# More blocks of an MLP by a seven-product scheme, both batches in turn to the last block

## The chip, the cores and the metric

One core of a Trainium2 chip runs the whole program. The time is the device time of one execution in microseconds (us); lower is better. Three runs of the kernel before gave a median of 463.32 us, from 462.43 to 463.98.

## The reference

Two batches of 768 tokens go through three parts. First a decaying linear attention over 8 heads of 64. Then a layer norm and an MLP whose result is added to its input. Then a mixture of four attention heads of width 64 of which each token uses two.

```
state = gamma * state + outer(k_t, v_t);  y_t = scale * q_t @ state      # 8 heads, 768 steps
xn = (x - mu) / sqrt(var + 1e-6) * g_ln
x  = x + maximum(xn @ w_ch1, 0) @ w_ch2                                   # 512 -> 2048 -> 512
logits = x @ w_gate;  w = softmax over the two largest of four
for e in range(4):
    q, k, v = x @ wq[e], x @ wk[e], x @ wv[e]
    a = softmax(causal(q @ k.T / 8))
    out += (weight of e) * (a @ v @ wo[e])
```

## The kernel before, in words

Everything is written as nodes of a plan (`P.add`): each has the engine, an estimated duration, what it reads and writes, and a priority, which is its place in the program plus `P.bias`. `P.issue` then runs a list scheduler over these estimates: at every step an engine that is free takes the ready node of the smallest priority number whose buffers have a place. The order that comes out is the order of the instructions on each engine, DMA issues on SP's queue included. A node that is ready late by the estimates is simply ordered later, and other work goes ahead of it.

Three stages follow each other. In the first (up to about 70 us) `r_tile` does the linear attention and the layer norm in 12 tiles of 128 tokens. Tokens are then kept transposed, features on partitions, in two halves of 384 tokens per batch (`j` = 0, 1): `xT` in fp32, and `XH` and `XL`, a rounded high part and the rest, since each product of full precision is done as three matmuls (high by high, high by low, low by high).

The second stage is the MLP, in eight blocks `f` of 256 hidden columns. For each block `m_h` makes the hidden values of one batch and one half in two groups of 12 matmuls of 128x384 (L576), ACT and DVE split the result (L579, L580), and `m_c` adds the block's part to `xT`: 6 matmuls (L595) and one DVE add (L598) for each of four groups of features. In the last block `m_c` also splits the new `xT` into `XH` and `XL` (L601, L603). The weights arrive as four pieces of 512 KB per block in 64-bit floats; `split_piece` turns them into fp32 on ACT, POOL and DVE (L508 to L514) and splits them (L532, L533), eight pieces ahead. Buffers of the weights hold two blocks.

Blocks in `SEVEN` (3, 4 and 5) use another way for the first product, `m_h7`: for one batch it takes both token halves and both weight halves as a 2x2 block product and makes the four results with seven products of 6 matmuls (L654) where `m_h` has eight. It needs sums of weight blocks (`w_sums`, L548 to L551, into two `S` buffers per block, of which four places exist, one shared with a `raw` buffer of the arriving weights) and sums of token blocks (`x_sums`, 12 POOL instructions L616, L619, L623 per batch, made once). Partial results are kept and added on ACT and DVE (L661, L665). The `m_c` groups of the batch before are put between the seven products.

The third stage: `load_mw` brings in wk, wq, wv and wo and splits them (L711 to L713); `q_proj` (L738) makes queries and keys, `q_val` (L775) values and gate logits, of batch 0 and later of batch 1; `a_scores`, `a_value`, `a_out` are the attention. `q_phase(1)` is there to fill the gaps of batch 0's attention.

Before, blocks 0 to 5 go through both batches in turn, and blocks 6 and 7 first for batch 0, then for batch 1. The loads of wk, wq, wv and wo are put into the plan at steps 20 to 23, in block 5, and wait for the last `m_h7`. `x_sums(0)` and `x_sums(1)` are put in at the first step of block 1 and of block 2, with a bias of 150.

Of the kernel before, what the change touches and what calls it, by code (L numbers as in the profile page):

```python
# [41 lines left out]
NB = S // TB  # L42
# [2 lines left out]
NFC = FF // FC  # L45
NPC = 4
LATE = 150
SEVEN = (3, 4, 5)
NEG = -1000000000.0
LIMIT = float(np.array(0x0FEFFFFF, np.uint32).view(np.float32))  # L50

# [155 lines left out]
def region(base, size, n, space="S"):  # L207
    return [(space, base + i * size, size) for i in range(n)]
# [3 lines left out]
def retention_channel_mlp_mixture_attention(ctx: ExitStack, tc: tile.TileContext, a):  # L212
# [71 lines left out]
    PL["u"] = region(o_u, 3 * KB // 2, 3) + region(o_w + 28 * KB, 3 * KB // 2, 2)  # L284
    PL["xT"] = region(o_xt, 6 * KB, 4)
    PL["x"] = region(o_x, 6 * KB, 8)
    x = o_r
    for n, size in (("wq", 4 * KB), ("wk", 4 * KB), ("wv", 4 * KB + 16), ("wo", 4 * KB)):
        PL[n] = region(x, size, 2)
        x += 2 * size  # L290
    PL["mraw"] = region(x, 4 * KB + 16, 2)
    PL["qk0"] = region(x, 3 * KB, 12)
    PL["vv0"] = region(x + 36 * KB, KB, 6)
    x += 42 * KB
    PL["ob"] = region(x, 2 * KB, 1) if x + 2 * KB <= o_h else []
    assert x <= o_h
    PL["qk1"] = region(o_h, 3 * KB, 12)
    PL["vv1"] = region(o_h + 36 * KB, KB, 6)
    PL["ob"] += region(o_h + 42 * KB, 2 * KB, 1)
    PL["pr"] = region(o_xt, 3 * KB, 8)  # L300
    PL["pt"] = region(o_x, 6 * KB, 3)
    PL["at"] = region(o_x + 18 * KB, 2 * KB, 3)
# [238 lines left out]
    def w_sums(f, y0, y1):  # L541
        t, h, l = new("sf"), new("S"), new("S")
        part = lambda i: f32(t)[:, 256 * i:256 * i + 256].rearrange("p (k c) -> p k c", k=2)
        for i, p, q, op in ((0, lambda: half_of(y0, 1), lambda: half_of(y1, 1), OP.add),
                            (1, lambda: part(0), lambda: half_of(y0, 0), OP.subtract),
                            (2, lambda: half_of(y0, 0), lambda: half_of(y0, 1), OP.subtract),
                            (3, lambda: half_of(y1, 0), lambda: part(1), OP.subtract)):
            P.add({"V": 0.45, "G": 0.8}, lambda e, i=i, p=p, q=q, op=op: (dve if e == "V" else pool).tensor_tensor(  # L548
                part(i), p(), q(), op), r=[y0, y1] + [(t, n) for n in {1: [0], 3: [1]}.get(i, [])], w=[(t, i)])
        ACT(1.1, lambda: act.activation(f32r(h), f32(t), AF.Copy), r=[(t, i) for i in range(4)], w=[h])  # L550
        P.add({"V": 1.2, "G": 2.4}, lambda e: (dve if e == "V" else pool).tensor_tensor(f32r(l), f32(t), f32(h), OP.subtract),  # L551
              r=[h] + [(t, i) for i in range(4)], w=[l])
        W[f, "S"] = (h, l)

    def w1_at(f, k, m):
        i, k = divmod(k, 2)
# [68 lines left out]
    def m_h7(f, b, rest):  # L625
        a11, (y1h, y1l), (sh, sl) = W[f, 0][0], W[f, 1], W[f, "S"]

        def weights(n):
            if n == "a11":
                return [a11], lambda k: (f32r(a11)[:, k * 128:(k + 1) * 128], f32r(a11)[:, 256 + k * 128:256 + (k + 1) * 128])  # L630
            h, l = (sh, sl) if n[0] == "s" else (y1h, y1l)
            c0 = 256 * int(n[1]) if n[0] == "s" else 128 * int(n[1])
            step = 128 if n[0] == "s" else FC
            return [h, l], lambda k: tuple(f32r(t)[:, c0 + k * step:c0 + k * step + 128] for t in (h, l))

        def tokens_of(n):
            if n[0] == "t":
                h, l = TH[b][int(n[1])], TL[b][int(n[1])]
                return [h, l], lambda k: tuple(f32r(t)[:, k * TB:(k + 1) * TB] for t in (h, l))
            kh, j = int(n[1]), int(n[2])  # L640
            h, l = XH[b][j], XL[b][j]
            return keys(h) + keys(l), lambda k: tuple(blk(f32r(t))[:, 2 * kh + k] for t in (h, l))

        def product(pa, wn, xn, first):
            wr, wat = weights(wn)
            xr, xat = tokens_of(xn)

            def mm():
                n = 0
                for k in range(2):  # L650
                    wh, wl = wat(k)
                    xh, xl = xat(k)
                    for wt, t in ((wh, xh), (wh, xl), (wl, xh)):
                        pe.matmul(f32(pa, TB), lhsT=wt, rhs=t, start=(first and n == 0), stop=(n == 5), skip_group_check=True)  # L654
                        n += 1
            r = [(t, z) for t in wr for z in (0, 1)] if wn == "a11" else list(wr)
            PE(1.04, mm, r=r + xr, w=[pa])

        def keep(pa):
            u = new("u")  # L660
            ACT(0.49, lambda: act.activation(f32(u), f32(pa, TB), AF.Copy), r=[pa], w=[u])  # L661
            return u

        def add(dst, pa, u):
            DVE(0.55, lambda: dve.tensor_tensor(f32(dst, TB), f32(pa, TB), f32(u), OP.add), r=[pa, u], w=[dst])  # L665

        def out(src):
            h, l = new("h"), new("h")
            ACT(0.49, lambda: act.activation(f32r(h, TB), f32(src, TB), AF.Relu), r=[src], w=[h])
            DVE(0.55, lambda: dve.scalar_tensor_tensor(f32r(l, TB), f32(src, TB), 0.0, f32(h, TB), op0=OP.max,  # L670
                                                       op1=OP.subtract), r=[src, h], w=[l])
            return h, l

        pa, pb, pc = (new("ps") for _ in range(3))
        def go_on(n=1):
            for _ in range(min(n, len(rest))):
                m_c(*rest.pop(0))

        product(pa, "a11", "x00", True)
        c1 = keep(pa)  # L680
        product(pb, "s1", "t1", True)
        add(pb, pb, c1)
        go_on()
        product(pa, "y0", "x10", False)
        h00 = out(pa)
        u2 = keep(pb)
        go_on()
        product(pc, "s0", "t0", True)
        go_on()
        product(pb, "s2", "t2", False)  # L690
        u3 = keep(pb)
        c22 = new("u")
        add(c22, pc, u3)
        go_on()
        product(pb, "y1", "t3", False)
        h10 = out(pb)
        go_on()
        product(pc, "s3", "x11", False)
        add(pc, pc, u2)
        h01 = out(pc)  # L700
        h11 = out(c22)
        P.writer["sums"] = P.nodes[-1]
        return [h00, h10], [h01, h11]

    MW = {}

    def load_mw(n):
        raw, h, l = new("mraw"), new(n), new(n)
        w = E * HD + E if n == "wv" else E * HD
        sz = NK * w  # L710
        DMA(sz * 512, lambda: sp.dma_start(f32(raw, sz), a[n].rearrange("p k n -> p (k n)")), r=["sums"], w=[raw])  # L711
        ACT(1.05, lambda: act.activation(f32r(h, sz), f32(raw, sz), AF.Copy), r=[raw], w=[h])
        POOL(2.4, lambda: pool.tensor_tensor(f32r(l, sz), f32(raw, sz), f32(h, sz), OP.subtract), r=[raw, h], w=[l])  # L713
        MW[n] = (h, l, DM if n == "wo" else w)
# [14 lines left out]
    def q_proj(b, j, n, p):  # L729
# [3 lines left out]
        for hf in range(2):  # L733
            def mm(hf=hf):
                i = 6 * hf
                for k in (2 * hf, 2 * hf + 1):
                    for lo, xt in ((0, xh), (0, xl), (1, xh)):
                        pe.matmul(f32(pa, TB), lhsT=mw(n, lo, k, p * 128, (p + 1) * 128), rhs=blk(f32r(xt))[:, k],  # L738
                                  start=(i == 0), stop=(i == 11))
                        i += 1  # L740
            PE(0.98, mm, r=list(MW[n][:2]) + xkeys(xh) + xkeys(xl), w=[pa])
        for z in range(2):
            e = 2 * p + z
            own = slice(64 * z, 64 * z + 64)
# [200 lines left out]
    DMA(8e3, lambda: sp.dma_start(before, a["before"]), w=["before"])  # L945
    DVE(0.1, lambda: dve.memset(negs, NEG), w=["negs"])
    steps = []
    for f in range(NFC - 2):
        steps += [(f, b, j) for j, b in (((0, 0), (0, 1), (1, 0), (1, 1)) if f == 0 else ((0, 0), (1, 0), (0, 1), (1, 1)))]
    for b in range(B):  # L950
        steps += [(f, b, j) for f in (NFC - 2, NFC - 1) for j in range(NB)]
    nxt = 8
    rest = []

# [4 lines left out]
    for n, (f, b, j) in enumerate(steps):  # L959
        for _ in range(2 if f >= NFC - 2 else 1):  # L960
            if nxt == len(pieces):
                break
            load_piece(*pieces[nxt])
            split_piece(*pieces[nxt])
            nxt += 1
        if (f, b, j) in ((1, 0, 0), (2, 0, 0)):
            P.bias += LATE
            x_sums(f - 1)
            P.bias -= LATE
        if n in (20, 21, 22, 23):  # L970
            load_mw(("wk", "wq", "wv", "wo")[n - 20])
        if f not in SEVEN:
            flush()
            hh = m_h(f, b, j)
            rest = [(f, b, j, hh, k) for k in range(NK)]
        elif j == 1:
            hs = m_h7(f, b, rest)
            flush()
            rest = [(f, b, jj, hh, k) for jj, hh in enumerate(hs) for k in range(NK)]

    flush()

    def q_phase(b):
# [83 lines left out]
```

## Time and profile before

| what | value |
|---|---|
| median of three runs | 463.32 us |
| the profiled execution | 464.56 us, its span 462.8 us |
| instructions | 8255 |
| DVE busy | 315.7 us (68%) |
| ACT busy | 217.4 us (47%) |
| POOL busy | 201.3 us (44%) |
| granted TensorE clock | 0.998 of full speed |
| PE's share of the chain that ended last | 86% |
| L595 and L576, shares of that chain | 27% and 18% |

The span is what lies between the first and the last instruction of the profile. PE is a matmul, PEld the load of its weights, which overlaps it; DVE, ACT and POOL are the vector, scalar and GpSimd engines, SP issues the DMAs. L595 is line 595 of the kernel as printed above.

### The profile page before, as it was taken

The numbers are of one execution on the slowest core, as the hardware profiler recorded it, in microseconds if no ns is written. First come the engines' busy times: TensorE is split into PE (matmuls) and PEld (weight loads), VectorE is DVE, ScalarE is ACT, GpSimd is POOL, SyncE is SP. The second block draws the span as 40 slices with busy tenths as digits, with TensorE's granted clock in tenths as the row PEclk, the third lists the DMA queues.
The fourth block names the chain that finished last, engine by engine and source line by source line (L and its number), as shares of the span: only waits on it lengthen the run. The fifth ranks groups of instructions, "written<-read, shape, count | busy, mean of one in ns | idle before, by whom it ended". The sixth has DMA issues, their size and how long they took to land.

```text
span 462.8 us, 8255 instructions
## 1 busy us (share of the span) xinstructions
PE 450.2 (97%) x3117; PEld 424.5 (92%) x3117; DVE 315.7 (68%) x671; ACT 217.4 (47%) x458; POOL 201.3 (44%) x209
## 2 busy tenths in 40 slices
PE   4999999999999999999999999999999999999996
PEld 4888899999999999999999999999899988898774
DVE  2697878667659559779988344443547888778962
ACT  0576685362255136255455212303434767745862
POOL 1588779889885123334145602202100514224440
PEclk9999999999999999999999999999999999999999
DMA  7899820333004005014214100000220231101111
GB/s 261 310 333 341 321 96 31 108 105 99 24 17 165 3 0 182 3 44 139 91 47 142 43 0 2 0 1 0 69 61 10 65 72 47 45 2 47 45 47 45
DMA packets 14983, 40.08 MB, mean 87 GB/s; under 512 B 2272, under 2 KB 4960, under 8 KB 14944
## 3 DMA queue, kind: packets, MB, share of 16 engines
q1 hardware_dynamic: 14944, 39.57, 25.3%
q8 instruction: 24, 0.39, 0.4%
q14 instruction: 15, 0.12, 0.1%
HBM read 33.27 MB, written 3.15 MB: 79 GB/s over the span
## 4 chain that ended last, share of the span: by engine, by line
PE 86%; DMA 3%; DVE 3%; ACT 3%; POOL 2%; issue 2%; SPq 0%; POOLq 0%; DVEq 0%; ACTq 0%
PE ps L595 27%; PE ps L576 18%; PE ps L654 8%; PE ps L738 6%; PE ps L891 4%; PE ps L775 4%; PE ps L880 4%; PE ps L910 4%; PE ps L838 2%; PE ps L839 2%; DMA raw<-in_w_dram 2%; PE ps L472 2%; PE ps L428 2%; PE ps L447 2%; PE ps L440 1%
## 5 line engine op out<-in xcount | busy, mean ns | idle before, releaser
L595 PE MATMUL ps<-h,w 128*128 128x384 f32 x768 | 141.8, 335 | 1.2 <-DVE xT L598 0.5
L595 PEld LDWEIGHTS ps<-h,w 128*128 128x128 f32 x768 | 133.6, 188 | 2.4 <-DVE xT L598 0.8
L598 DVE TENSOR_TENSOR xT<-xT,ps 128x384 f32<-128x384 f32 x128 | 69.7, 551 | 31.9 <-PE ps L595 31.6
L576 PE MATMUL ps<-x,w 128*128 128x384 f32 x480 | 86.8, 335 | 0.0
L576 PEld LDWEIGHTS ps<-x,w 128*128 128x128 f32 x480 | 83.3, 188 | 0.0
L860 POOL TENSOR_SCALAR pr<-pr,sm,gate 128x384 f32<-128x384 f32 (+5 forms) x48 | 34.8, 734 | 83.5 <-DVE ps L845 34.6
L579 ACT ACTIVATE h<-ps 128x384 fp32r<-128x384 f32 x40 | 19.6, 491 | 76.1 <-PE ps L576 76.1
L533 POOL TENSOR_TENSOR w<-wy,w 128x512 fp32r<-128x512 f32 x29 | 37.6, 1307 | 40.6 <-ACT w L532 22.2
L580 DVE SCALAR_TENSOR_TENSOR h<-ps,h 128x384 fp32r<-128x384 f32 x40 | 22.1, 556 | 42.3 <-ACT h L579 42.3
L848 ACT ACTIVATE pr<-ps,sm 128x384 f32<-128x384 f32 (+5 forms) x48 | 30.3, 635 | 16.6 <-DVE sm L846 10.5
L603 POOL TENSOR_TENSOR x<-xT,x 128x384 fp32r<-128x384 f32 x11 | 11.2, 1017 | 56.5 <-ACT x L601 56.3
L509 POOL TENSOR_SCALAR wx<-wx 128x512 f32<-128x512 f32 x32 | 20.2, 632 | 34.4 <-ACT wx L508 32.0
L508 ACT ACTIVATE wx<-raw 128x512 f32<-128x512 f32 x32 | 21.5, 672 | 27.4 <-DVE ps L512 16.6
L846 DVE TENSOR_REDUCE sm<-ps 128x1 f32<-128x384 f32 (+5 forms) x48 | 30.0, 625 | 2.8
L532 ACT ACTIVATE w<-wy 128x512 fp32r<-128x512 f32 x29 | 17.8, 627 | 11.1 <-PE ps L595 8.1
L512 DVE SCALAR_TENSOR_TENSOR ps<-wx,ps 128x512 uint32<-128x512 uint32 x32 | 22.2, 693 | 0.9
L514 DVE SCALAR_TENSOR_TENSOR wy<-raw,ps 128x512 uint32<-128x512 uint32 x32 | 21.7, 683 | 1.3 <-POOL w L533 0.6
L510 DVE TENSOR_SCALAR ps<-wx 128x512 uint32<-128x512 uint32 x32 | 22.0, 687 | 0.8
L880 PE MATMUL ps<-ident,pr 128*128 128x128 f32 x168 | 22.0, 275 | 0.1
L432 DVE TENSOR_TENSOR am<-ps,caus 128x512 f32<-128x512 f32 x24 | 15.6, 684 | 9.3 <-PE ps L428 9.1
L838 PE MATMUL ps<-qk,qk 128*128 128x512 f32 (+3 forms) x64 | 21.7, 347 | 0.2 <-ACT pr L848 0.2
L654 PE MATMUL ps<-t,S 128*128 128x384 f32 x108 | 21.5, 334 | 0.0
(115 smaller groups left out, 803.9 us busy)
## 6 DMA issues: line engine op xcount, KB each, us to landing
raw<-in_w_dram SPq DMA_DIRECT2D x32, 512.0 KB, 3.6
vk<-in_vk_dram SPq DMA_DIRECT2D x12, 512.0 KB, 5.6
kq<-in_kq_dram SPq DMA_DIRECT2D x11, 512.0 KB, 6.1
qk<-qk SPq DMA_DIRECT2D x32, 96.0 KB, 2.1
out_dram<-ob SPq DMA_DIRECT2D x11, 256.0 KB, 2.0
tabY<-in_tabY_dram SPq DMA_DIRECT2D x6, 256.0 KB, 5.1
mraw<-in_wv_dram SPq DMA_DIRECT2D x1, 520.0 KB, 3.3
kq<-in_kq_dram SPq DMA_DIRECT2D x2, 256.0 KB, 3.2
```

Source lines behind the costliest of these rows:

```text
L512: DVE(0.7, lambda: dve.scalar_tensor_tensor(u32(z), u32(x), 0x80000000, u32(z), op0=OP.bitwise_and, op1=OP.bitwise_or), r=[x, z], w=[z])
L533: POOL(1.34, lambda: pool.tensor_tensor(f32r(l), f32(y), f32(h), OP.subtract), r=[y, h], w=[l])
L576: pe.matmul(f32(pa, TB), lhsT=wt, rhs=blk(f32r(xt[b][j]))[:, k], start=(n == 0), stop=(n == 11))
L595: pe.matmul(f32(pa, TB), lhsT=wt, rhs=t, start=(n == 0), stop=(n == 5))
L598: DVE(0.55, lambda k=k, pa=pa: dve.tensor_tensor(blk(f32(xt))[:, k], blk(f32(xt))[:, k], f32(pa, TB), OP.add), r=[pa] + keys(xt), w=[(xt, ...
L654: pe.matmul(f32(pa, TB), lhsT=wt, rhs=t, start=(first and n == 0), stop=(n == 5), skip_group_check=True)
L738: pe.matmul(f32(pa, TB), lhsT=mw(n, lo, k, p * 128, (p + 1) * 128), rhs=blk(f32r(xt))[:, k], start=(i == 0), stop=(i == 11))
L838: pe.matmul(f32(s)[:, n0:n1], lhsT=q, rhs=f32r(KH[b, e])[:, n0:n1], start=True, stop=False)
L846: dve.tensor_reduce(f32(sm)[:, z:z + 1], f32(s, nk), axis=AX, op=OP.max, negate=True)
L848: ACT(act_c(nk) + .18, lambda s=s, pr=pr, z=z: act.activation(f32(pr, nk), f32(s, nk), AF.Exp, bias=f32(sm)[:, z:z + 1], scale=1.0, accum_ ...
L860: POOL(0.28 + nk * 0.95e-3, lambda pr=pr, z=z, e=e: pool.tensor_scalar(f32(pr, nk), f32(pr, nk), f32(sm)[:, 6 + z:7 + z], GT[b, j][:, cc, ...
L880: pe.transpose(f32(pa)[:, i * C:(i + 1) * C], f32(PRS[z][x])[:, j * C:(j + 1) * C], ident)
```

## The change

`SEVEN` becomes blocks 2 to 7. The steps are f = 0 to 7, in each of them both batches. `x_sums` of batch 0 is put in within block 0 and that of batch 1 at the start of block 1, with the same bias. wk and wq are put in at two steps of block 7 and wait for the last block's weight sums; wv and wo are put in behind the last step and wait for the last `m_h7` (key `"seven"`), and so does every `q_proj`. The third stage's buffers get other places, since token and weight sums now live to the end: wk, wq and wo share six places, wv's two parts lie where the raw loads of the others lie, and wv's raw load lies on the `u` buffers.

```diff
@@ -45,7 +45,7 @@
 NFC = FF // FC
 NPC = 4
 LATE = 150
-SEVEN = (3, 4, 5)
+SEVEN = (2, 3, 4, 5, 6, 7)
 NEG = -1000000000.0
 LIMIT = float(np.array(0x0FEFFFFF, np.uint32).view(np.float32))
 
@@ -284,19 +284,17 @@
     PL["u"] = region(o_u, 3 * KB // 2, 3) + region(o_w + 28 * KB, 3 * KB // 2, 2)
     PL["xT"] = region(o_xt, 6 * KB, 4)
     PL["x"] = region(o_x, 6 * KB, 8)
-    x = o_r
-    for n, size in (("wq", 4 * KB), ("wk", 4 * KB), ("wv", 4 * KB + 16), ("wo", 4 * KB)):
-        PL[n] = region(x, size, 2)
-        x += 2 * size
-    PL["mraw"] = region(x, 4 * KB + 16, 2)
-    PL["qk0"] = region(x, 3 * KB, 12)
-    PL["vv0"] = region(x + 36 * KB, KB, 6)
-    x += 42 * KB
-    PL["ob"] = region(x, 2 * KB, 1) if x + 2 * KB <= o_h else []
-    assert x <= o_h
+    slots = region(o_r + 48 * KB, 4 * KB, 6)
+    for n in ("wk", "wq", "wo"):
+        PL[n] = slots
+    x = o_h - 2 * (4 * KB + 16)
+    PL["wv"] = PL["mraw"] = region(x, 4 * KB + 16, 2)
+    PL["vraw"] = region(o_u, 4 * KB + 16, 1)
+    PL["qk0"] = region(o_r, 3 * KB, 12)
+    PL["vv0"] = region(o_r + 36 * KB, KB, 6)
+    PL["ob"] = region(o_r + 42 * KB, 2 * KB, 2)
     PL["qk1"] = region(o_h, 3 * KB, 12)
     PL["vv1"] = region(o_h + 36 * KB, KB, 6)
-    PL["ob"] += region(o_h + 42 * KB, 2 * KB, 1)
     PL["pr"] = region(o_xt, 3 * KB, 8)
     PL["pt"] = region(o_x, 6 * KB, 3)
     PL["at"] = region(o_x + 18 * KB, 2 * KB, 3)
@@ -551,6 +549,7 @@
         P.add({"V": 1.2, "G": 2.4}, lambda e: (dve if e == "V" else pool).tensor_tensor(f32r(l), f32(t), f32(h), OP.subtract),
               r=[h] + [(t, i) for i in range(4)], w=[l])
         W[f, "S"] = (h, l)
+        P.writer["sums"] = P.nodes[-1]
 
     def w1_at(f, k, m):
         i, k = divmod(k, 2)
@@ -699,16 +698,16 @@
         add(pc, pc, u2)
         h01 = out(pc)
         h11 = out(c22)
-        P.writer["sums"] = P.nodes[-1]
+        P.writer["seven"] = P.nodes[-1]
         return [h00, h10], [h01, h11]
 
     MW = {}
 
     def load_mw(n):
-        raw, h, l = new("mraw"), new(n), new(n)
+        raw, h, l = new("vraw" if n == "wv" else "mraw"), new(n), new(n)
         w = E * HD + E if n == "wv" else E * HD
         sz = NK * w
-        DMA(sz * 512, lambda: sp.dma_start(f32(raw, sz), a[n].rearrange("p k n -> p (k n)")), r=["sums"], w=[raw])
+        DMA(sz * 512, lambda: sp.dma_start(f32(raw, sz), a[n].rearrange("p k n -> p (k n)")), r=["seven" if n in ("wv", "wo") else "sums"], w=[raw])
         ACT(1.05, lambda: act.activation(f32r(h, sz), f32(raw, sz), AF.Copy), r=[raw], w=[h])
         POOL(2.4, lambda: pool.tensor_tensor(f32r(l, sz), f32(raw, sz), f32(h, sz), OP.subtract), r=[raw, h], w=[l])
         MW[n] = (h, l, DM if n == "wo" else w)
@@ -738,7 +737,7 @@
                         pe.matmul(f32(pa, TB), lhsT=mw(n, lo, k, p * 128, (p + 1) * 128), rhs=blk(f32r(xt))[:, k],
                                   start=(i == 0), stop=(i == 11))
                         i += 1
-            PE(0.98, mm, r=list(MW[n][:2]) + xkeys(xh) + xkeys(xl), w=[pa])
+            PE(0.98, mm, r=list(MW[n][:2]) + xkeys(xh) + xkeys(xl) + ["seven"], w=[pa])
         for z in range(2):
             e = 2 * p + z
             own = slice(64 * z, 64 * z + 64)
@@ -945,10 +944,8 @@
     DMA(8e3, lambda: sp.dma_start(before, a["before"]), w=["before"])
     DVE(0.1, lambda: dve.memset(negs, NEG), w=["negs"])
     steps = []
-    for f in range(NFC - 2):
+    for f in range(NFC):
         steps += [(f, b, j) for j, b in (((0, 0), (0, 1), (1, 0), (1, 1)) if f == 0 else ((0, 0), (1, 0), (0, 1), (1, 1)))]
-    for b in range(B):
-        steps += [(f, b, j) for f in (NFC - 2, NFC - 1) for j in range(NB)]
     nxt = 8
     rest = []
 
@@ -963,12 +960,12 @@
             load_piece(*pieces[nxt])
             split_piece(*pieces[nxt])
             nxt += 1
-        if (f, b, j) in ((1, 0, 0), (2, 0, 0)):
+        if (f, b, j) in ((0, 0, 1), (1, 0, 0)):
             P.bias += LATE
-            x_sums(f - 1)
+            x_sums(f)
             P.bias -= LATE
-        if n in (20, 21, 22, 23):
-            load_mw(("wk", "wq", "wv", "wo")[n - 20])
+        if n in (28, 30):
+            load_mw("wk" if n == 28 else "wq")
         if f not in SEVEN:
             flush()
             hh = m_h(f, b, j)
@@ -978,6 +975,8 @@
             flush()
             rest = [(f, b, jj, hh, k) for jj, hh in enumerate(hs) for k in range(NK)]
 
+    load_mw("wv")
+    load_mw("wo")
     flush()
 
     def q_phase(b):
```

## Rows read from the trace of the kernel before

**Rows 1.** The page: busy time of the engines, share of the span, instructions.
```profile
PE 450.2 (97%) x3117; PEld 424.5 (92%) x3117; DVE 315.7 (68%) x671; ACT 217.4 (47%) x458; POOL 201.3 (44%) x209
```
**Rows 2.** Windows: PE, PEld, DVE, ACT, POOL busy (instructions), clock, DMA share, GB/s.
```profile
126.90:161.30 34.40, 34.40 (x201) 34.37 (x200) 24.21 (x41) 13.96 (x25) 17.49 (x15) 1.00 0.18 62
161.30:194.20 32.90, 32.59 (x188) 32.27 (x187) 25.31 (x45) 14.53 (x29) 10.40 (x10) 1.00 0.19 64
194.20:227.00 32.80, 32.30 (x187) 31.98 (x186) 26.50 (x45) 16.05 (x32) 10.64 (x11) 1.00 0.29 96
227.00:259.90 32.90, 32.80 (x189) 32.51 (x188) 25.82 (x48) 16.62 (x30) 16.09 (x11) 1.00 0.25 81
259.90:291.00 31.10, 31.10 (x181) 31.10 (x181) 12.11 (x22) 6.54 (x13) 5.99 (x6) 1.00 0.01 2
```
**Rows 3.** Pieces of the chain of waits: start, length, line.
```profile
81.32 6.24 PE ps L576 x36
...
165.58 1.04 PE ps L654 x6
```
**Rows 4.** Waits of PE and PEld: total, times, longest, in us.
```profile
PE ps L595 <- DVE xT L598: 0.5, 1, 0.5
...
PE ps L595 <- DVE h L670: 0.3, 1, 0.3
```
**Rows 5.** Groups of instructions of DVE that the seven products add.
```profile
L665 DVE TENSOR_TENSOR ps<-ps,u 128x384 f32<-128x384 f32 x12 | 6.7, 561 | 1.2 <-PE ps L654 1.2
...
L551 DVE TENSOR_TENSOR S<-sf,S 128x1024 fp32r<-128x1024 f32 x2 | 3.0, 1500 | 0.0
```
**Rows 6.** Instructions of line 548: duration min/median/max in ns, first and last start.
```profile
L548 DVE TENSOR_TENSOR sf<-sf,wy x3: 1054/1392/1395, 141.5 to 209.8; 128x256 f32<-128x256 f32 x3
...
L548 DVE TENSOR_TENSOR sf<-wy,sf x3: 409/416/716, 142.9 to 211.2; 128x256 f32<-128x256 f32 x3
```
**Rows 7.** Timeline: start, length, line; token sums, second block and first seven products.
```profile
72.63 1.84 POOL L616 TENSOR_TENSOR t<-x,x 128x768 f32<-128x768 f32 x1
...
105.71 3.65 POOL L623 TENSOR_TENSOR t<-t,t 128x768 fp32r<-128x768 f32 x2
...
124.84 4.32 PE L576 MATMUL ps<-x,w 128*128 128x384 f32 x24
...
142.99 2.07 POOL L623 TENSOR_TENSOR t<-t,t 128x768 fp32r<-128x768 f32 x1
```
**Rows 8.** Timeline between blocks 3 and 4: release of a weight sum's buffer.
```profile
185.77 1.20 PE L654 MATMUL ps<-x,S 128*128 128x384 f32 x6
...
186.88 2.40 POOL L551 TENSOR_TENSOR S<-sf,S 128x1024 fp32r<-128x1024 f32 x1 [0.93 <-PE ps L654]
...
189.93 1.20 PE L654 MATMUL ps<-t,S 128*128 128x384 f32 x6
```
**Rows 9.** Timeline: end of the MLP, first values of batch 0.
```profile
326.75 2.38 PE L595 MATMUL ps<-h,w 128*128 128x384 f32 x12 [0.29 <-DVE qk L757]
...
338.18 1.72 PE L775 MATMUL ps<-wv,x 128*128 128x260 f32 x12
```
**Rows 10.** Loads of the third stage: landing in us, splits, differences of the last block.
```profile
mraw<-in_wv_dram SPq DMA_DIRECT2D x1, 520.0 KB, 3.3
...
L712 ACT ACTIVATE wv<-mraw 128x1040 fp32r<-128x1040 f32 x1 | 1.1, 1077 | 0.9 <-DMA mraw<-in_wv_dram 0.9
...
L713 POOL TENSOR_TENSOR wv<-mraw,wv 128x1040 fp32r<-128x1040 f32 x1 | 2.4, 2427 | 0.9 <-ACT wv L712 0.9
...
L713 POOL TENSOR_TENSOR wo<-mraw,wo 128x1024 fp32r<-128x1024 f32 x1 | 2.4, 2399 | 1.3 <-ACT wo L712 1.3
...
L603 POOL TENSOR_TENSOR x<-xT,x 128x384 fp32r<-128x384 f32 x11 | 11.2, 1017 | 56.5 <-ACT x L601 56.3
```
**Rows 11.** Windows of line 738 alone, first scores to first transposes: PE, PEld.
```profile
353.30:368.70 15.40, 12.34 (x66) 11.58 (x66) 1.00 0.14 33
```

## The prediction

> **What bounds the kernel now.** The page comes first. PE is busy for 97% of the span and PEld for 92%, DVE for 68% [rows 1], so the first question is whether DVE or a wait bounds PE in some stage. The windows answer it stage by stage: from 126.9 to 161.3 us PE and PEld are busy for the whole stretch, in the three windows to 259.9 us, where the seven products run, PE misses 0.31, 0.50 and 0.10 us, and from 259.9 to 291 us it misses nothing while DVE has 12.11 us of work in 31.10 [rows 2]. Next the chain of waits, to see that these busy times are the engine at its pace: 36 matmuls in a row take 6.24 us and 6 take 1.04, with L576 as with L654 [rows 3], 0.1733 us each. Of PE's waits in the MLP the longest are on DVE, 0.5 us for an add and 0.3 us for a hidden value [rows 4]. So in the blocks that change, a matmul less is 0.173 us less, as long as no new wait opens.
>
> **What goes.** For one batch `m_h` has 48 matmuls in a block (2 halves, 2 groups, 12 each), `m_h7` has 42. Blocks 2, 6 and 7 change, two batches each: 3 x 2 x 6 = 36 matmuls, just the piece of 6.24 us [rows 3]. I take -6.24 us.
>
> **What the three blocks get.** ACT has 6 copies to `u` more per block and one copy of sums, POOL trades one difference of 512 columns for two of 256; neither is near its limit in rows 2. DVE gets 6 adds at 0.561 us, 3.4 us, then the weight sums, and the low part of these at 1.50 us [rows 5]. The sums: three adds between 0.41 and 1.39 us each [rows 6], so 1.2 to 4.2 us. Per block that is 3.4 + 1.5 + 1.2 to 4.2 = 6.1 to 9.1 us; the sums come one block ahead. Block 2: 24.21 + 3.4 = 27.6 of 34.40 - 2.08 = 32.3 us, the sums for block 3 being in that window already. Block 5, which now makes the sums for block 6: 25.82 + 2.7 to 5.7 = 28.5 to 31.5 of 32.9 us. Block 6 has room, 12.11 in 31.10 us for batch 0 alone [rows 2]. DVE stays under PE everywhere, but bursts let PE wait, as the three windows with seven products show: 0.91 us in all. I take the same again for the three new blocks, +0.91 us; one end is 3 x 0.50 = 1.5 us, the other -0.91, if with the new order of the plan the old gaps go too (the window before them, with one block's sums in it, loses nothing).
>
> The Trainium skill says on this ("SBUF — State Buffer", section "Who interferes with whom") that a VectorE instruction with two SBUF inputs excludes a GpSimd instruction that reads SBUF and the reverse, for the whole instruction. This trace agrees: the same shape takes 409 ns at best and 1395 at worst [rows 6]. By that rule alone each of the four two-input instructions of a block's sums could wait for one token sum of 1.84 us [rows 7], 7.4 us of DVE; where that would end is the first rival.
>
> **The buffers of the weight sums.** `S` has four places, one shared with a weight load, so the next block's low part waits until the last product of the block before has read its own. Between blocks 3 and 4 one sees it: the product at 185.77 us, the low part on POOL at 186.88 for 2.40 us after a wait on PE, and the first product that reads it at 189.93 [rows 8]. It is done at 189.28, with 0.65 us to spare, because `m_c` groups and a product that needs no sums lie between. The change makes two more such turns, into block 3 and into block 6; for block 7 no weight load holds the shared place. I take 0 for each, by that row; the other end is a low part with nothing ahead of it, 2.40 us each.
>
> **The token sums.** All 24 POOL instructions must now end before blocks that start one block (some 33 us) sooner. Before, batch 0's start at 72.63 us and end at 109.36; block 2's products start in the middle of the piece at 124.84, at 126.9 [rows 7]. So batch 0 has 17 us to spare. Batch 1's last ends at 145.06 [rows 7]. Its seven products follow 7 products and 8 `m_c` groups of 1.04 us after 126.9, at 142.5, and the first that reads a token sum comes a product later, near 143.5, and reads the second of four sums; the fourth is read by the sixth product, near 150. With the queueing as it was the loss would be at most 1.5 us; queued sooner, ahead of block 3's differences, I take 0. The reverse, POOL's tile work being held up by a token sum, is bounded by one of 1.84 us; PE was busy with products of block 0 there, so 0.
>
> **The end of the MLP.** Batch 0's queries could start before, but the plan started them only as the last product groups ended: the MLP's last matmuls are at 326.75 us, and the first values of batch 0 at 338.18 [rows 9]. So that batch 0 was finished early was hardly used, and little is lost by waiting for `"seven"`: behind the last product PE has 8 `m_c` groups, 8.3 us, for which the hidden values of the first half are long ready, and then 8 `q_proj` of 2.08 us, 16.6 us. Behind these 24.9 us lie the loads of wv and wo, which come late now: 3.3 us to landing, 1.08 us for the high part, then, since wo's raw load has taken the second of wv's two places, wo's difference of 2.40 us and wv's of 2.43 [rows 10]; with wo's own landing behind wv's I make it 11 to 12 us. Even if POOL first does the 8 differences of batch 1's last block at 1.02 us [rows 10], it is 20 us. SP's queue has only transfers of keys behind these issues, which are no earlier. wk and wq are loaded in block 7, with POOL nearly idle. I take 0, between -0.3 (the wait at 326.75 goes [rows 9]) and the price of the third rival.
>
> **Sum.** -6.24 + 0.91 = -5.33 us. Against the profiled execution, 464.56 us with 1.76 us of it outside the span, that is 459.2; this execution lay 1.24 us above the median of 463.32, so the predicted median is 458.0 us. With the ends of the small terms it is 463.32 - 6.24 - 0.91 - 0.3 = 455.9 to 463.32 - 6.24 + 1.5 (blocks) + 1.5 (token sums) = 460.1; the turns of `S` are the first rival.
>
> **Rivals.** First, weight sums come too late: both new turns of `S` lose their 2.40 us, because DVE and POOL hold each other up in the sums (the short add was lengthened to more than three times [rows 6]). -5.33 + 4.8 = -0.5, 462.8 us, no measurable change. For it: only 0.65 us to spare [rows 8]. Against it: no wait of PE on a weight sum is among its waits in three blocks. That is where the Trainium skill's rule on the shared port would end.
>
> Second, the time is given back in part: the list scheduler orders the third stage anew, and PE loses 2 to 3 us among scores and transposes, 460.5 us. For it: DVE has little slack there. Against it: the stage's work is the same.
>
> Third, slower: the values of batch 0 come late. Until gates and values are there no transposes and value products can go, and PE uses the queries and keys of batch 1 meanwhile. These were the filling between the first scores and the first transposes, 66 matmuls [rows 11]; spent earlier, they leave up to 66 x 0.173 = 11.4 us of PE open, 458.0 + 11.4 = 469.4 us. It decides from the point where wv's low part is later than 24.9 us after the last `m_h7`, for instance if POOL does wo, wv and all the last differences in the wrong order; by the sum above there are 5 to 13 us in hand.
>
> Fourth, the change doesn't do what it says: the products stay away from PE's path, and it is 463.3. The chain, with PE on 36 matmuls in 6.24 us, speaks against it.
>
> **Chances.** Forecast 0.66, the second rival 0.12 (all but a part of it faster), the first 0.10, the third 0.10, the fourth 0.02. A measurement of this kernel can tell about 0.3%, 1.4 us. Faster, below 461.9: forecast and second rival, 0.78 less a little, 0.77. The same: 0.12. Slower, above 464.7: the third rival and a bit more, 0.11. The range goes from 455.8, the lower end above, to 462.8, where the first rival stands; it leaves out the third and fourth, 0.12, and the tails of the others.
>
> **What would show it.** Right: line 654 with 504 matmuls in place of 252 and the MLP's last matmul some 5 us before its old place, PE busy over 98% in block 2 and blocks 6 and 7, the stage from there to the end as long as before within 1 us. Wrong: PE waiting on `S` (L550, L551) or `t` (L622, L623) in blocks 2, 3 and 6, or a gap of PE, or `q_proj` of batch 1, where the values of batch 0 stood.

## The result, and the profile after

| kernel | median, us | runs | ratio to before, 95% interval |
|---|---|---|---|
| before | 463.35 | 462.43 to 463.98 | |
| after | 459.6 | 458.19 to 460.04 | 0.9914 (0.9894 to 0.9934) |
| after, measured again beside 17 runs of before (463.55) | 459.27 | 458.17 to 460.33 | 0.9906 (0.9889 to 0.9923) |

The change makes the kernel 0.9% faster, some 4 us; 458.0 was predicted, and the 459.6 lies inside the predicted range, 455.8 to 462.8. The profiled execution took 459.39 us, its span 457.3. First the engines' line of the page after, which answers to [rows 1]:

```profile
PE 442.7 (97%) x3081; PEld 417.1 (91%) x3081; DVE 336.1 (73%) x701; ACT 228.4 (50%) x479; POOL 208.8 (46%) x212
```

36 matmuls are gone from PE (3117 to 3081), and DVE has 20.4 us more. The windows after, columns as in [rows 2]; the first holds most of block 2's seven products, each of the next four reaches from the second batch of one of blocks 3 to 6 to that of the next, and the last is the second batch of block 7:

```profile
126.90:154.00 27.10, 26.77 (x154) 26.45 (x153) 20.48 (x37) 14.34 (x28) 18.50 (x14) 1.00 0.23 79
...
169.60:201.30 31.70, 31.48 (x181) 31.16 (x181) 25.62 (x45) 14.42 (x28) 10.40 (x10) 1.00 0.20 67
201.30:233.30 32.00, 31.50 (x183) 31.18 (x182) 25.82 (x45) 13.86 (x28) 10.46 (x10) 1.00 0.19 66
233.30:265.30 32.00, 31.51 (x182) 31.19 (x182) 24.52 (x43) 13.31 (x27) 9.84 (x9) 1.00 0.15 51
265.30:297.00 31.70, 31.49 (x182) 31.17 (x181) 20.85 (x36) 13.11 (x26) 10.57 (x7) 1.00 0.10 34
297.00:320.90 23.90, 23.90 (x139) 23.90 (x138) 16.46 (x31) 12.08 (x25) 8.36 (x8) 1.00 0.13 45
```

PE misses 0.33, 0.22, 0.50, 0.49 and 0.21 us, one wait in the second batch of each of blocks 2 to 6, 1.75 us against 0.91 in [rows 2]. The waits of PE after, which answer to [rows 4]:

```profile
PE ps L594 <- DVE xT L597: 1.4, 4, 0.5
PE ps L737 <- DVE qk L756: 0.9, 1, 0.9
...
PE ps L594 <- DVE h L669: 0.3, 1, 0.3
```

All five are waits on DVE, none on a weight sum or a token sum. The sixth, 0.9 us, stands at the first queries and keys. DVE's sums after, two of their groups, which answer to [rows 6]:

```profile
L546 DVE TENSOR_TENSOR sf<-sf,wy x6: 425/1393/1508, 106.5 to 271.6; 128x256 f32<-128x256 f32 x6
...
L546 DVE TENSOR_TENSOR sf<-wy,sf x6: 407/570/1401, 108.4 to 273.0; 128x256 f32<-128x256 f32 x6
```

The plan reckons 0.45 us for each. What one of the five costs is more than its row. PE's timeline after, around the fifth product of block 4's second batch (start, length, line):

```profile
207.56 1.20 PE L594 MATMUL ps<-h,w 128*128 128x384 f32 x6
208.59 1.21 PE L653 MATMUL ps<-t,S 128*128 128x384 f32 x6
210.30 2.35 PE L594 MATMUL ps<-h,w 128*128 128x384 f32 x12 [0.50 <-DVE xT L597]
212.50 1.20 PE L653 MATMUL ps<-t,w 128*128 128x384 f32 x6
```

From 208.59 to 212.50 are 3.91 us for 18 matmuls that take 3.12 at pace: 0.79 us lost, where the row says 0.50. Two things are not in the row. A group of 6 is listed with 1.20 us where the next starts 1.04 after it, so 0.17 us of the gap is listed as busy; and the 12 behind the gap take 2.20 us to the start of the next group, 0.12 more than at pace. Read from start to start, the five waits lost 3.2 us, and the three of before 1.7. On DVE the add that PE waits for (L597) stands behind the sums, which hold DVE from 207.19 to 209.79:

```profile
207.64 1.40 DVE L546 TENSOR_TENSOR sf<-sf,wy 128x256 f32<-128x256 f32 x1
209.07 0.72 DVE L546 TENSOR_TENSOR sf<-wy,sf 128x256 f32<-128x256 f32 x1
209.71 0.54 DVE L597 TENSOR_TENSOR xT<-xT,ps 128x384 f32<-128x384 f32 x1
```

To compare kernels I use three such stretches: from the start of the last transposes of the first stage (L470, in before L472) to the first `q_proj`, from there to the first scores, and from there to the end of the span. For before, where the first `q_proj` lay ahead of the last `m_c`, the first two go together.

| kernel | first stage to | MLP | to the scores | to the end |
|---|---|---|---|---|
| before | 74.47 | 278.80 (both) | | 109.53 |
| after | 73.88 | 247.03 | 26.98 | 109.41 |
| after, again | 73.68 | 247.03 | 27.01 | 109.48 |

After has 274.01 us where before has 278.80: -4.79, and the stretch to the end is the same. The first stage, by this mark, ends anywhere between 72.4 and 74.8 us in the profiles of this case.

### The profile page after: what moved, and what is told of

Same layout as the page of the kernel before. It is cut to its first block, busy times and chain, and to the rows that moved or that the text cites. A ratio compares the mean times of both kernels' runs of the same rounds, so it can differ in the third digit from the quotient of the medians.

```text
span 457.3 us, 8243 instructions
## 1 busy us (share of the span) xinstructions
PE 442.7 (97%) x3081; PEld 417.1 (91%) x3081; DVE 336.1 (73%) x701; ACT 228.4 (50%) x479; POOL 208.8 (46%) x212
## 4 chain that ended last, share of the span: by engine, by line
PE 80%; DVE 5%; DMA 5%; ACT 3%; issue 3%; POOL 2%; SPq 0%; POOLq 0%; DVEq 0%; ACTq 0%
PE ps L594 25%; PE ps L653 15%; PE ps L575 7%; PE ps L737 6%; PE ps L890 4%; PE ps L879 4%; PE ps L774 4%; PE ps L909 4%; DMA kq<-in_kq_dram 3%; PE ps L837 2%; PE ps L838 2%; DVE sf L546 2%; PE ps L445 2%; PE ps L426 2%; PE ps L470 2%
## 5 line engine op out<-in xcount | busy, mean ns | idle before, releaser
L594 PE MATMUL ps<-h,w 128*128 128x384 f32 x768 | 145.9, 336 | 1.7 <-DVE xT L597 1.4
L597 DVE TENSOR_TENSOR xT<-xT,ps 128x384 f32<-128x384 f32 x128 | 69.3, 550 | 29.1 <-PE ps L594 28.9
L531 POOL TENSOR_TENSOR w<-wy,w 128x512 fp32r<-128x512 f32 x26 | 34.4, 1333 | 56.2 <-PE ps L594 34.8
L653 PE MATMUL ps<-t,S 128*128 128x384 f32 x216 | 43.3, 335 | 0.0
L653 PEld LDWEIGHTS ps<-t,S 128*128 128x128 f32 x216 | 38.0, 188 | 0.0
L660 ACT ACTIVATE u<-ps 128x384 f32<-128x384 f32 x36 | 17.5, 487 | 37.8 <-PE ps L653 31.0
L575 PE MATMUL ps<-x,w 128*128 128x384 f32 x192 | 35.0, 336 | 0.0
L575 PEld LDWEIGHTS ps<-x,w 128*128 128x128 f32 x192 | 33.3, 188 | 0.0
L653 PE MATMUL ps<-x,w 128*128 128x384 f32 x144 | 28.8, 335 | 0.0
L530 ACT ACTIVATE w<-wy 128x512 fp32r<-128x512 f32 x26 | 16.2, 628 | 24.1 <-PE ps L594 18.6
L668 ACT ACTIVATE h<-ps 128x384 fp32r<-128x384 f32 x36 | 17.6, 488 | 18.8 <-PE ps L653 9.4
L653 PEld LDWEIGHTS ps<-x,w 128*128 128x128 f32 x144 | 25.3, 188 | 0.0
L669 DVE SCALAR_TENSOR_TENSOR h<-ps,h 128x384 fp32r<-128x384 f32 x36 | 19.9, 552 | 4.8 <-ACT h L668 4.8
```

The lines of the kernel that those rows point to most:

```text
L531: POOL(1.34, lambda: pool.tensor_tensor(f32r(l), f32(y), f32(h), OP.subtract), r=[y, h], w=[l])
L575: pe.matmul(f32(pa, TB), lhsT=wt, rhs=blk(f32r(xt[b][j]))[:, k], start=(n == 0), stop=(n == 11))
L594: pe.matmul(f32(pa, TB), lhsT=wt, rhs=t, start=(n == 0), stop=(n == 5))
L597: DVE(0.55, lambda k=k, pa=pa: dve.tensor_tensor(blk(f32(xt))[:, k], blk(f32(xt))[:, k], f32(pa, TB), OP.add), r=[pa] + keys(xt), w=[(xt, ...
```

## The experiments

All were compared with the kernel before on the same chip.

**The change again.** No edit.

> The changed kernel once more, to narrow its time. Account from the two traces: 36 matmuls less are -6.24 us, PE's waits in the MLP rose from 0.91 to 1.75 us (+0.84), the waits at the first queries and keys from 0.46 to 0.93 us (+0.5): -4.9 us, a ratio of 0.989 to 0.990. The rival is that the timed difference of -3.75 us is the true one and the profiled executions (464.56 and 459.39, -5.17) differ by chance: 0.992.

Ratio 0.9906 (0.9889 to 0.9923), 459.27 us, between the two. By the stretches above both profiled executions agree to 0.03 us up to the scores and to 0.07 behind them, so the -4.79 us are steady. They differ by 0.2 us in the first stage; where the rest of the spread between runs lies is not shown.

**All of the change but the three blocks.**

```diff
-SEVEN = (2, 3, 4, 5, 6, 7)
+SEVEN = (3, 4, 5)
...
             nxt += 1
+            if nxt == len(pieces):
+                P.writer["sums"] = P.nodes[-1]
```

> The whole change but with seven products in blocks 3, 4 and 5 only: order of the batches, early token sums, late loads and buffers are those of the change. If the products are the whole gain and the rest costs only the half us at the first queries, it is 463.5 to 464.0 us (ratio to before 1.000 to 1.002). Rival: the order of the batches or of the third stage by itself brings or costs more than 1.5 us, below 462 or above 465.

The second edit lets the loads of wk and wq wait for the split of the last weights, since the last block has no sums here.

463.95 us, ratio 1.001 (0.9998 to 1.0022). The order of the batches, the early token sums, the late loads and the new places are together worth nothing; the gain is that of the products.

**Weight sums on POOL.**

```diff
-            P.add({"V": 0.45, "G": 0.8}, lambda e, i=i, p=p, q=q, op=op: ...
+            P.add({"G": 0.8}, lambda e, i=i, p=p, q=q, op=op: ...
...
-        P.add({"V": 1.2, "G": 2.4}, lambda e: ...
+        P.add({"G": 2.4}, lambda e: ...
```

> All weight sums on POOL, which is idle for half of blocks 2 to 7, none on DVE. If the waits of PE in each block (0.21 to 0.50 us, 1.75 in all) come from DVE being late by the sums, which a POOL instruction at the same time stretches from 0.42 to 1.40 us, they fall below 0.6 us and the time by 1.0 to 1.5 us against the changed kernel (ratio to before 0.986 to 0.988). Rival: they come from the conversion of the weights on DVE (0.69 us each, 12 a block) and stay above 1.2 us; or POOL's chain of 5.4 us brings the low part too late and PE waits on the weight sums, up to 2.4 us a block, slower than the changed kernel.

456.48 us (456.35 to 456.67), ratio 0.9847 (0.9832 to 0.9862): 2.8 us better than the change, about twice what was expected. The MLP takes 244.70 us in place of 247.03, -2.33, for the five waits are gone and one on ACT has come. That kernel's waits of PE in the MLP and behind it:

```profile
PE ps L737 <- DVE qk L756: 1.0, 1, 1.0
PE ps L653 <- ACT u L660: 0.6, 1, 0.6
```

I had expected less since I took the waits by their rows, 1.75 us, and not by the 3.2 they cost. The new wait on ACT costs 0.85 us from start to start, so 2.33 us are left in the MLP; the rest of the 2.8 us lies in front of it (73.47 in place of 73.7 to 73.9) and outside the span (1.9 us in place of 2.1).

**The last block's differences on POOL.**

```diff
-            P.add({"V": 0.47, "G": 1.0}, lambda e, k=k: ...
+            P.add({"G": 1.0}, lambda e, k=k: ...
```

> The differences of the last block (L602) on POOL only. In the changed kernel one of them took 2.47 us on DVE instead of 0.56 while POOL made wo's low part (2.39 us), and PE waited 0.93 us for a key behind it. If that is the cause, the 0.93 us go to under 0.3 and the time falls by 0.6 to 0.9 us (ratio to before about 0.002 below that of the changed kernel). Rival: POOL, with five differences of 1.02 us more, brings wv's low part later, the values of batch 0 start later and the time is the same or longer by up to 1 us.

459.77 us, ratio 0.9912 (0.9895 to 0.9929): no change in the time, against what was expected. The cause of the wait was right: the wait at the first queries falls from 0.93 to 0.2 us and that stretch from 26.98 to 26.28. But the stretch from the scores to the end is 110.01 in place of 109.41, which takes it back; whether the edit does that is not shown, for in the other profiles (but the one with wv late) this stretch lies anywhere between 109.4 and 109.8. The timeline of the changed kernel shows the cause of the wait:

```profile
322.24 2.39 POOL L712 TENSOR_TENSOR wo<-mraw,wo 128x1024 fp32r<-128x1024 f32 x1
322.57 2.47 DVE L602 TENSOR_TENSOR x<-xT,x 128x384 fp32r<-128x384 f32 x1 [0.80 <-ACT x L600]
...
324.97 1.13 DVE L756 TENSOR_TENSOR qk<-ps,qk 64x384 fp32r<-64x384 f32 x2
...
326.16 4.43 PE L737 MATMUL ps<-x,wq 128*128 128x384 f32 x24 [0.93 <-DVE qk L756]
```

The difference on DVE, 0.56 us elsewhere, ends 0.4 us after POOL's, the keys behind it start late, and PE waits.

**Idle work on DVE in the place of the sums.** Sums on POOL, and in their old place three or six memsets that the plan reckons at 1.35 us in both.

```diff
...
+        idle = new("idle")
+        for _ in range(3):                         # or 6, at 0.225
+            DVE(0.45, lambda: dve.memset(f32(idle), 0.0), r=[y0, y1], w=[idle])
```

> Weight sums on POOL as before, and in their old place on DVE three memsets of 400 columns a block that nobody needs (about 0.4 us each, 1.2 us, which is also what the plan reckons). If DVE held up PE because its sums ran longer than planned (0.42 us alone, 1.40 beside a POOL instruction), work of the planned length does no harm: 456.5 to 457.2 us, one wait of PE at most in blocks 2 to 7. Rival: any 1.2 us more on DVE at this place makes PE wait, 458 us or more.

455.98 us, ratio 0.9853 (0.9832 to 0.9875), as with no memsets; the MLP takes 244.70 us to the hundredth.

> The same with six memsets, 2.4 us, as long as the three stretched sums of the changed kernel were on DVE, while the plan still reckons 1.35 us for all; order of PE as in the run with three. If sums longer than planned are the cause of PE's waits, they come back in most blocks: 1.0 to 1.8 us above the run with three, about 458 to 459 us. Rival: the waits came from the chain of the sums themselves (their buffer, the wait for them), which stays on POOL here, and both runs are the same within 0.4 us.

462.0 us, ratio 0.9964 (0.995 to 0.9978); the MLP takes 249.96 us. Four waits on DVE are back, worse than expected: one of 0.52 us in block 2, and three of 1.07 us at the same matmuls of blocks 4, 5 and 6 where the changed kernel has its own. In block 3 there is none. The timeline of this kernel, at the place shown above:

```profile
207.60 0.39 DVE L551 MEMSET idle<- 128x400 f32 x1
...
210.31 0.39 DVE L551 MEMSET idle<- 128x400 f32 x1
210.62 0.49 DVE L601 TENSOR_TENSOR xT<-xT,ps 128x384 f32<-128x384 f32 x1
...
211.16 1.31 PE L598 MATMUL ps<-h,w 128*128 128x384 f32 x6 [1.07 <-DVE xT L601]
```

Each memset takes 0.39 us, but they start 0.54 apart, so the six hold DVE for 3.1 us where the stretched sums held it for 2.6 (207.19 to 209.79 in the changed kernel). Three of them hold it for 1.5 us, near the 1.35 of the plan, and PE does not wait. The order of PE's instructions is the same in both runs. So the waits come from DVE work longer than the plan reckons, not from any work at that place, nor from the chain of the sums, which stayed on POOL. That six are also more work than three is settled by the next run.

**The plan told a truer duration.**

```diff
-            P.add({"V": 0.45, "G": 0.8}, lambda e, i=i, p=p, q=q, op=op: ...
+            P.add({"V": 1.0, "G": 0.8}, lambda e, i=i, p=p, q=q, op=op: ...
```

> The changed kernel, but the plan reckons 1.0 us for a weight sum on DVE in place of 0.45, near what they take beside POOL (0.42 to 1.40). If PE's waits come from sums longer than planned, the plan now puts other DVE work ahead of PE's needs or takes POOL for the sums, and the time falls by 1 to 2.5 us against the changed kernel, 457 to 458.3 us. Rival: the waits are a matter of DVE's total load in the block and stay, 459.4.

455.73 us, ratio 0.9837 (0.9823 to 0.9852), better than expected. 18 of the 24 sums are still on DVE, where it was 19. Five of them still take 1.39 to 1.51 us, where it was six, and all together 13.4 us, where it was 15.9; two groups of them in this run:

```profile
L546 DVE TENSOR_TENSOR sf<-sf,wy x6: 424/1392/1508, 105.9 to 268.3; 128x256 f32<-128x256 f32 x6
...
L546 DVE TENSOR_TENSOR sf<-wy,sf x5: 410/412/417, 107.8 to 238.9; 128x256 f32<-128x256 f32 x5
```

Yet PE has no wait left in the MLP, which takes 243.81 us, 3.22 less than in the changed kernel: just what its five waits had lost from start to start. The timeline of this run shows what the plan did, at the place in block 4 shown above:

```profile
205.91 1.39 DVE L546 TENSOR_TENSOR sf<-sf,wy 128x256 f32<-128x256 f32 x1
207.22 0.54 DVE L597 TENSOR_TENSOR xT<-xT,ps 128x384 f32<-128x384 f32 x1
207.69 0.41 DVE L546 TENSOR_TENSOR sf<-wy,sf 128x256 f32<-128x256 f32 x1
```

The add that PE needs now goes ahead of the last sum. The rival, DVE's load, falls: here the three sums take 2.22 us of DVE and PE does not wait, where in blocks 3 and 6 of the changed kernel 2.24 and 2.23 us cost it 0.22 and 0.21 us by the rows. DVE's busy time in the whole kernel, 331.8 us, is lower by 4.3 us; what decides is that the order reckons with the longer sums.

**The kernel before with its sums on POOL.** The edit of the weight sums, made to the kernel before.

> The kernel before with its weight sums on POOL alone. If the stretched sums on DVE cost each seven-product block a wait, its three blocks lose three waits too (PE's rows from start to start lose 0.6 to 0.8 us at each of two, 0.3 at the third, 1.7 us in all): 461.6 to 462.4 us, ratio 0.996 to 0.998. The seven products in blocks 2, 6 and 7 are then worth the difference to the run with sums on POOL in six blocks (456.5), 5.1 to 5.9 us, near the 6.24 of their matmuls. Rival: nothing here, 463.6.

461.75 us, ratio 0.9968 (0.9954 to 0.9982), as expected: its three blocks lost 1.7 us in the same way, 277.03 us from the first stage to the scores in place of 278.80. The seven products in three more blocks, with no wait on DVE in the MLP on either side, are 277.03 against 243.81 + 27.00 = 270.81 us of the run before this one: 6.22 us, which is the 36 matmuls. At the queries and keys the small waits on both sides lose nearly the same, some 1.5 us.

**The token sums sooner.**

```diff
-LATE = 150
+LATE = 0
```

> The bias of the token sums is 0 instead of 150, so they go on POOL ahead of the later weights' differences and end sooner. The prediction costed their queueing at 0, since they end some us before they are read: the same as the changed kernel within 0.5 us. Rival: they did hold up block 2 or block 1's weights, and it moves by over 1 us either way.

457.73 us, ratio 0.9873 (0.9856 to 0.9891), 1.5 to 1.9 us better than the change: the rival. The MLP takes 246.38 us in place of 247.03; the wait on a hidden value in block 2 (0.3 us in the waits after) is gone. Of the rest, 0.6 to 0.8 us lie in the first stage, which ended at 73.09, and 0.3 outside the span (1.8 us in place of 2.1); whether that is the edit or chance is not settled.

**wv late.**

```diff
-        DMA(sz * 512, lambda: sp.dma_start(f32(raw, sz), ...), r=[...], w=[raw])
+        for _ in range(7 if n == "wv" else 1):
+            DMA(sz * 512, lambda: sp.dma_start(f32(raw, sz), ...), r=[...], w=[raw])
```

> wv is loaded seven times over before it is used, so that its low part comes some 20 us later than in the changed kernel, behind the end of batch 0's queries and keys. This is the third rival of the prediction on purpose: batch 1's queries and keys are used up before batch 0's transposes can start, up to 11.4 us of PE open, 464 to 470 us. The other theory: the list scheduler puts scores of batch 0 in front and keeps enough of batch 1's queries and keys for later, under 2 us lost, 460 to 461.5 us.

464.63 us, ratio 1.0028 (1.0014 to 1.0042), about 5 us slower than the change: the third rival's mechanism is real, at somewhat under half of its bound. wv's low part is ready at 350.16, 22.8 us later than in the changed kernel. PE's timeline of this run:

```profile
339.52 0.33 PE L838 MATMUL ps<-qk,qk 128*128 128x384 f32 x1
...
351.91 8.88 PE L775 MATMUL ps<-wv,x 128*128 128x260 f32 x72 [1.31 <-ACT pr L848]
...
367.96 0.63 PE L880 MATMUL ps<-ident,pr 128*128 128x128 f32 x4 [1.63 <-DVE qk L750]
```

The first scores come 8 us sooner than in the changed kernel, the values 19 us later, and batch 1's queries and keys are spent between them: PE then waits, 1.31 us ahead of the values and 1.63 ahead of the first transposes among others.

**Together.** Sums on POOL and token sums sooner, then the last differences on POOL as well.

> Sums of weights on POOL and the bias of the token sums 0. The token sums queued sooner brought 1.7 us in the changed kernel by the runs, of which the traces show 0.65 us in the MLP; if that adds to the 2.8 us of the sums on POOL it is 454.8 to 456.0 us, if the same wait of PE is meant 456.5 us.

456.48 us, ratio 0.9853 (0.9835 to 0.987): by the runs nothing added. The MLP is 243.84 us, 0.86 less than with the sums on POOL alone, but this run's first stage ended at 74.74, 1.3 us later, and 0.3 us more lie outside the span (2.2 us). So the trace shows a gain that the time does not.

> The same, and the differences of the last block on POOL alone as well. In the changed kernel that closed PE's wait of 0.93 us at the first queries but gave it back later (no change in the time). Expected again: within 0.5 us of the run without it. Rival: with less queued on DVE the wait closes for good, 0.7 us better.

454.26 us (453.97 to 455.14), ratio 0.9807 (0.9792 to 0.9823), the best kernel here, 2.2 us better, not within half a us. The stretch to the scores is 26.28 against 27.05, and the one to the end, 109.37, is 0.2 us shorter too, so here nothing is taken back: some 1.0 us. Why it was in the changed kernel stays open. The rest is the first stage again, 72.57 against 74.74 in the two profiled executions, which lie further apart (3.1 us) than the medians. Its page has PE at 98%:

```profile
PE 441.6 (98%) x3081; PEld 417.4 (92%) x3081; DVE 313.1 (69%) x673; ACT 229.6 (51%) x479; POOL 231.2 (51%) x240
```

## Why the prediction was right, and what it mis-sized

**What goes.** Right: PE was the bound and stayed it. With the DVE waits out of the MLP of both kernels the 36 matmuls measure 6.22 us. The signs came as named: L653 has 504 matmuls, and PE misses at most 1.2% of the windows that hold blocks 2, 6 and 7. Only the MLP's last matmul ends 8 us sooner (321.07 against 329.13) and not 5, since no queries stand between the last groups any more.

**What the three blocks get.** The mechanism was right, DVE bursts, one wait a block. The size was not: the term of +0.91 measures +1.45 (-4.79 + 6.24), since I read the windows' idle time of PE, which leaves out some 0.3 us at each gap, and since five waits came where three had been. Also the step set DVE's load against PE's; the runs with memsets and with the truer duration show that it is not the load but the difference from the plan's reckoning that opens the gaps. On the shared port the Trainium skill ("SBUF — State Buffer", "Who interferes with whom") was borne out further: the same difference on DVE takes 0.56 us alone and 2.47 beside POOL's 2.39. But its price came as waits on DVE's other work, and not, as in the first rival, as waits on the sums themselves.

**The weight sums' buffers.** Right at 0, but with less in hand than the row promised. The new turn into block 3, from POOL's and PE's timelines after:

```profile
149.84 1.20 PE L653 MATMUL ps<-x,S 128*128 128x384 f32 x6
150.96 2.40 POOL L549 TENSOR_TENSOR S<-sf,S 128x1024 fp32r<-128x1024 f32 x1 [1.82 <-PE ps L653]
154.00 1.20 PE L653 MATMUL ps<-x,w 128*128 128x384 f32 x6
155.04 1.20 PE L653 MATMUL ps<-t,S 128*128 128x384 f32 x6
```

It ends at 153.36, 1.7 us ahead of its reader; before it was 0.65 [rows 8]. The new turn into block 6 is closer:

```profile
248.88 2.40 POOL L549 TENSOR_TENSOR S<-sf,S 128x1024 fp32r<-128x1024 f32 x1 [3.07 <-PE ps L653]
251.75 1.20 PE L653 MATMUL ps<-t,S 128*128 128x384 f32 x6
```

That is 0.47 us to spare, and the turns into blocks 4 and 5 have 0.47 as well. So the first rival did not come, but only half a us lay between it and a first wait.

**The token sums.** They were never waited for: batch 1's last begins on POOL at 138.95 for 1.86 us, its reader at 147.76. But their queueing was not worth 0; with a bias of 0 the MLP is 0.65 us shorter.

**The end of the MLP.** The loads kept clear of the values: by POOL's timeline wv's low part is ready at 327.32, 17.7 us behind the last of the seven products (309.59), within the 11 to 20 worked out, and the first values come at 332.94, 12.0 us after the first queries and keys. What lies before them was worked out wrong: between 309.44 and 332.94 PE had 11 groups of `m_c` and 5 of `q_proj` (66 and 60 matmuls), not 8 and 8, so there were some 23.3 us and not 24.9, and 5.6 us in hand, the low end of the 5 to 13. One thing was missed: a late load's split on POOL stretches a difference on DVE, 0.93 us of PE. By luck, for neither was reckoned, it was nearly paid for by small waits that went: from the first queries and keys to the first values PE loses 1.6 us (12.03 us for 60 matmuls at 0.1733), before it was 1.5 (16.04 us for 84).

**Sum.** By the trace -4.8 to -4.9 us, against -5.33: 0.5 us is the term of +0.91. Another 0.3 us lies outside the span, which the prediction left at 1.76 us: the time is longer than the span by 2.07 to 2.17 us in the nine executions of after and by 1.75 to 1.82 in the 17 of before that were measured beside five of them. With seven products in blocks 3 to 5 only it is 1.74 to 1.84, but with the token sums sooner 1.77 to 1.83, all three new blocks kept; what makes it is not shown. Measured again, where 463.55 - 5.33 = 458.2 meets 459.27, the two make up most of the difference. What is left of the 1.6 us between 458.0 and 459.6 lies within the spread of the runs.

**Rivals.** The first did not come, as above. The second did not: scores to end take 109.41 against 109.53. The third is real but was not met: it cost about 5 us with wv 22.8 us later; from what delay on it costs anything was not tried. The fourth is out with the 36 matmuls.

## What to carry to other kernels

Read what a gap on TensorE costs from start to start of the work around it, not from its idle column: here some 0.3 us more each. Where an order is planned from estimated durations, an instruction that runs longer than its estimate can cost the bound engine time even if its own engine has room; correct the estimate, or move it to an engine where it is steady (on POOL the sums took 0.73 to 0.75 us). Here one number of the plan brought 3.2 us in the MLP by the traces and 3.5 to 3.9 by the times, two thirds and more of what the change itself brought.

## What the runs showed of the hardware

Six memsets on DVE that write the same buffer start 0.54 us apart though each takes 0.39. And the first stage, which no edit was aimed at, ended between 72.43 and 74.77 us in fourteen profiles; PE waits there for the loads of keys and queries, 4.7 us in before and 5.0 in after by the waits of PE; what moves it was not tried.
